# Batch 2 of a dilated sliding-window attention: crossing all eight heads by DMA and computing them in four quadrant visits

## The chip, the cores and the metric

The kernel runs on one core of a Trainium2 chip. A core has a matrix engine (PE, with its weight loads shown apart as PEld), a vector engine (DVE), a scalar engine (ACT), a general engine (POOL) and a sync engine (SP), each with its own instruction queue that is worked off strictly in order. POOL and SP also start DMA transfers. The metric is the device time of one execution in microseconds (us); lower is better. The kernel before takes 291.92 us, the median of 3 runs (291.9 to 294.13).

## What is computed

The input is q, k and v of shape (8 batches, 8 heads, 576 positions, 64) and two weight matrices. Heads 0 to 3 attend to the last 32 positions, heads 4 to 7 to every fourth of the last 128. The result, as a 4608 by 512 matrix, goes through a feed-forward layer with squared ReLU.

```python
rel = pos[:, None] - pos[None, :]
mask_plain = (rel >= 0) & (rel < window)                                        # window = 32, heads 0..3
mask_dil = (rel >= 0) & (rel < window * dilation) & (rel % dilation == 0)       # dilation = 4, heads 4..7
scores = np.where(masks, scale * np.matmul(q, k.transpose(0, 1, 3, 2)), -1e9)
attn = softmax(scores)
x = np.matmul(attn, v)            # then (batch, position) by (head, dim): 4608 x 512
h = np.maximum(x @ w_in, 0.0)     # 512 x 2048
out = h * h @ w_out               # 2048 x 512
```

## The kernel before, in words

Everything is written out by hand in one order, and each engine takes its share of that order. The backbone is the feed-forward layer. Its PE work is cut into groups, numbered g = 0, 1, 2 and so on. Tokens come in tiles: four tiles of 256 tokens with 16 groups each (groups 0 to 63), then tiles of 512 tokens with 32 groups each (from group 64). Of the tile of tokens 768 to 1023, groups 48 to 55 are the first product (line 912, eight results u0 to u7), groups 56 to 63 the second (line 960). Each result of a first product sits in one of the four PSUM buffers called pf until ACT evicts it with the ReLU (line 925); DVE then squares it (line 930 or 889). A matmul of a later result waits for the buffer of the result four before.

Between the groups stand the steps of the attention. Batches and heads are counted from 0, so the third batch is batch 2 (the name XB in the code) and the fourth is batch 3 (NATURAL). Two heads form a pair e: pairs 0 and 1 are plain, 2 and 3 dilated. Two lists say what is issued behind which group: PROGRAM, whose cells between the bars belong to one group each, and the list `steps`, sorted by group and then by a small priority.

The batches are treated in different ways. Batch 1 is transposed on PE: a code such as 1q2 (line 284) turns q of pair 2 into PSUM, and copies spread it into qT and, block by block, into the block-diagonal key tile kbd (lines 304 to 321). Codes a and b compute scores, exponential and mask of a pair's two parts (lines 358 to 369), o and p its value product and normalisation (lines 421 to 436); a digit in front is the batch. From batch 3 on nothing is transposed on PE. Four DMA transposes on SP (line 264, code x) bring q and k of all heads into the tiles qx and kx; copies put them where PE wants them (`arrange`: R, the ends of the dilated pairs; K, the plain pairs' keys; Q, their queries), and PE then works in four quadrants of its array at once, in visits (line 621, code V: pairs for scores, then pairs for values). After a visit come E (exponential on ACT, line 658, then mask on DVE), L (logarithm of the sums on ACT, lines 634 to 640) and X (exponential of its negative on ACT, line 644, then the products on DVE, lines 647 and 649). A visit with values of one pair is followed by four logarithms, one with values of two pairs by two for each.

Batch 2 is a mixture before the change. Its dilated heads are crossed by DMA and computed in quadrants: V022,23 for the scores behind group 56, and the value products with the next batch's first scores behind group 59. Its plain pairs are transposed on PE (2q0, 2k0, 2q1, 2k1) and computed by a, b, o and p behind groups 39 to 56.

The loads come from POOL in the order of the codes L: q and k (line 197), v (codes p, d and r, lines 218 to 239). Eight semaphores are used in turn, so that a load waits for the one eight before it. SP's queue holds the DMA transposes and the stores of results (line 852), also in order.

The two lines below, from `quadrants` and the group's eviction, show the shared buffers:

```python
main_s = [ps_a.tile([P, 512], f32, name="pa") for _ in range(2)]
nc.scalar.activation(hv, acc[u][:, :].rearrange("p (x n) -> p x n", x=2), ACT.Relu)
```

Of the kernel before, what the change touches and what calls it, by code (L numbers as in the profile page):

```python
# [12 lines left out]
RES = 4  # L13
# [68 lines left out]
def kernel(  # L82
# [118 lines left out]
    def crossed(b: int, e: int):  # L201

        return int(b == XB and e == 3 or b >= NATURAL and e == 1)

    def load_v(b: int, parts, which="pdr"):
# [8 lines left out]
        for what in which:  # L214
            if what == "p":
                for e in range(NE // 2):
                    for hl, rows in sides:
                        nc.gpsimd.dma_start(  # L218
                            dst[rows, e, i0:i1, rows],
                            v[b, 2 * e + hl, 64 * i0 : 64 * i1, :].rearrange("(i p) d -> p i d", p=64),  # L220
                        )
# [14 lines left out]
            elif b == XB:  # L236
                for g, rows in sides:
                    for i in (0, 8):
                        nc.gpsimd.dma_start(
                            dst[rows, NE // 2 : NE, i, rows],  # L240
                            v[b, H // 2 + g : H - g : 3 - 2 * g, 64 * i : 64 * i + 64, :].rearrange("h p d -> p h d"),
# [19 lines left out]
    def cross(b: int, nm: str, part: int):  # L261

        n, m0, h0 = MN[part], MS[part], H // 2 if b == XB else 0
        nc.sync.dma_start_transpose(
            (qx if nm == "q" else kx)[b % 2][:, h0:, :, m0 : m0 + n].rearrange("p h c m -> p (h c) m"),
            staged(b, nm)[0:n, part, h0:, :].rearrange("p h x -> p (h x)"),
        )

    def trans(b: int, e: int, nm: str, part: int, home: str):
# [5 lines left out]
        if b == 2:  # L275
            m0, n, pitch, cuts = 0, M, M, [(t[0:80, a, :, :], MS[a], 80) for a in range(2)]
        else:

            m0, n, pitch, cuts = MS[part], MN[part], 80, [(t[0:80, part, :, :], 0, 80)]
# [160 lines left out]
    def step(b: int, code: str):  # L440
# [6 lines left out]
        if what in "qk" and (b > XB or b == XB and e >= NE // 2):  # L447
            t = (qx if what == "q" else kx)[b % 2]
            halves(e, what, t[:, 2 * e : 2 * e + 2, :, :], 0, M, copier(what, e, home), his)
        elif what in "qQkK" and "h" in home:  # L450
# [37 lines left out]
    def arrange(b: int, what: str, g: int, jj: int, copy=nc.vector.tensor_copy):  # L488
# [6 lines left out]
        if what == "Q":  # L495
            nc.vector.tensor_copy(q_both[rows, :, jj::2, :], qx[b % 2][src, 0:n, :, :])
# [126 lines left out]
    def natural_step(b: int, code: str):  # L623
# [28 lines left out]
        else:  # L652
# [6 lines left out]
            mask = (mask_f if e >= NE // 2 else mask_n)[:, 0:n]  # L659
# [207 lines left out]
    def ffn_groups(tk0: int, nt: int):  # L867
# [7 lines left out]
        kts = (2, 3, 0, 1) if tk0 >= 3 * NT else (0, 2, 1, 3) if NT <= tk0 < 2 * NT else (0, 1, 2, 3) if tk0 in (0, 2 * NT) else (2, 3, 0, 1)  # L875
# [271 lines left out]
    def run(code):  # L1147
        if code == "y":
            for nm in "qk":
                nc.gpsimd.memset(staged(1, nm)[64:80, 0, :, :], 0.0)  # L1150
                nc.gpsimd.memset(staged(2, nm)[64:80, 0, 0 : H // 2, :], 0.0)
# [40 lines left out]
    COMBINE = {17: "10", 18: "20", 22: "11 21", 61: "40", 62: "41", 63: "30 31"}  # L1192
# [11 lines left out]
    for x, code in enumerate(("R00", "R01", "R10", "R11")):  # L1204
        steps.append((48 + x, 1, XB, code))
    steps.append((56, 2, XB, "V022,23/"))
# [83 lines left out]
```

## Time and profile before

| what | value |
|---|---|
| median of 3 runs | 291.92 us (291.9 to 294.13) |
| profiled execution, whole | 292.3 us |
| its span | 290.5 us |
| instructions in the span | 8181 |
| DMA | 83125 packets, 35.45 MB, mean 122 GB/s |
| stage of batch 2, groups 40 to 63 | 60.21 to 88.94 us of the span |

The span runs from the first to the last instruction of one profiled execution; the time of a run is a little longer. Each line of the profile that is quoted below names an engine, a line of the kernel, the operation, and the tile written from the tile read. In a timeline the first column is the start in us of the span, the second the time from the first start to the last end of the instructions that the row merges, and xN their number; what stands in square brackets is idle time of the engine ahead of them. In a list of groups the columns after the count are busy time in us, mean duration of one in ns, and idle time ahead. Instructions of one engine overlap a little, so a row's cost is often read from one start to the next.

### The profile page before, as it was taken

Reading aid. Unit: us, or ns where it says so; the run is one execution under the profiler, and the core shown is the slowest. Engines: PE = TensorE matmul, PEld = TensorE weight load, DVE = VectorE, ACT = ScalarE, POOL = GpSimd, SP = SyncE. Lnnn points to the kernel's source line nnn. Section 1 sums busy time; section 2 is a strip of 40 time slices with the busy share of each in tenths; the row PEclk is TensorE's granted clock in tenths of the full one; section 3 lists DMA queues with packets and bytes.
Section 4 is the critical chain, followed back from the end, with each engine's and each line's share of the span. In section 5 each row is a group of like instructions: output and inputs, shape, how many; then the busy total and the mean of one; then the engine's idle time right before and its main releaser. Section 6 shows DMA issues by size and latency. Waiting matters only on the chain.

```text
span 290.5 us, 8181 instructions
## 1 busy us (share of the span) xinstructions
PE 280.7 (97%) x3321; PEld 200.4 (69%) x3341; DVE 207.0 (71%) x447; ACT 194.7 (67%) x419; POOL 130.0 (45%) x210
## 2 busy tenths in 40 slices
PE   8879999999999999999999999999999999999994
PEld 3569855977955578557865786578657865885683
DVE  2565496798877997869786978697869545742762
ACT  7688748877986886597669766976697456306610
POOL 8569965393892779584043467950000000000000
PEclk9999999999999999999999999999999999999999
DMA  7999999999999987999789998740310040013013
GB/s 112 200 158 212 210 159 201 211 157 200 164 152 179 153 113 80 230 207 132 97 146 215 164 162 163 82 27 2 101 47 2 2 148 0 0 47 100 0 38 108
DMA packets 83125, 35.45 MB, mean 122 GB/s; under 512 B 52624, under 2 KB 78480, under 8 KB 83088
## 3 DMA queue, kind: packets, MB, share of 16 engines
q0 software_dynamic: 49280, 18.43, 55.9%
q1 hardware_dynamic: 33008, 16.10, 27.9%
q10 hardware_dynamic: 800, 0.41, 0.6%
q8 instruction: 26, 0.43, 0.6%
q14 instruction: 11, 0.09, 0.1%
HBM read 37.40 MB, written 9.44 MB: 161 GB/s over the span
## 4 chain that ended last, share of the span: by engine, by line
PE 88%; DMA 5%; DVE 2%; POOL 2%; issue 1%; ACT 1%; ACTq 0%; POOLq 0%
PE pf L912 41%; PE pf L997 29%; PE pf L960 8%; DMA w_in<-in_moe_w_in_dram 3%; DMA kb<-in_k_dram 2%; PE po L621 2%; PE pa L621 1%; PE pa L284 1%; PE pf L621 1%; PE pd L621 1%; POOL qb L197 1%; PE pa L358 1%; PE po L421 1%; DVE kbd L507 1%; PE pd L423 0%
## 5 line engine op out<-in xcount | busy, mean ns | idle before, releaser
L912 PE MATMUL pf<-xT,w_in 128*128 128x512 bf16 (+1 forms) x693 | 128.7, 340 | 2.1 <-DMA w_in<-in_moe_w_in_dram 1.4
L912 PEld LDWEIGHTS <-w_in 128*128 128x128 bf16 x704 | 77.4, 113 | 46.1 <-DMA w_in<-in_moe_w_in_dram 1.5
L925 ACT ACTIVATE h2T<-pf 128x512 bf16<-128x512 f32 x144 | 83.0, 600 | 36.7 <-PE pf L912 36.4
L997 PEld LDWEIGHTS <-h2T 128*128 128x128 bf16 x688 | 65.3, 98 | 9.1
L997 PE MATMUL pf<-w_out_sb,h2T 128*128 128x256 bf16 x440 | 52.3, 273 | 0.0
L483 POOL DMA_DIRECT2D vbd<-in_v_dram x80 | 43.4, 564 | 13.6 <-DMA qb<-in_q_dram 4.2
L889 DVE TENSOR_TENSOR h2T<-h2T 128x2048 bf16<-128x2048 bf16 (+2 forms) x42 | 35.6, 867 | 16.2 <-ACT h2T L925 15.6
L1008 DVE TENSOR_TENSOR osb<-pf,osb 128x512 f32<-128x512 f32 (+1 forms) x35 | 23.5, 673 | 12.6 <-PE pf L997 11.8
L960 PE MATMUL pf<-w_out_sb,h2T 128*128 128x512 bf16 x119 | 29.5, 379 | 0.6 <-issue 0.3
L647 DVE TENSOR_TENSOR xT<-po,rec 128x512 bf16<-128x512 f32 x16 | 11.0, 688 | 15.8 <-ACT rec L644 11.2
L197 POOL DMA_DIRECT2D qb<-in_q_dram x18 | 13.1, 730 | 16.3 <-DMA xx<-qb 15.0
L960 PEld LDWEIGHTS <-h2T 128*128 128x128 bf16 x128 | 11.4, 98 | 10.8
L930 DVE TENSOR_TENSOR h2T<-h2T 128x1024 bf16<-128x1024 bf16 (+1 forms) x20 | 11.5, 585 | 7.7 <-ACT h2T L925 7.2
L658 ACT ACTIVATE pt<-pa 128x384 bf16<-128x384 f32 (+1 forms) x32 | 15.3, 496 | 1.7 <-DVE xT L649 1.1
L475 POOL DMA_DIRECT2D vbd<-in_v_dram x20 | 12.3, 626 | 8.4 <-DMA kb<-in_k_dram 4.2
L644 ACT ACTIVATE rec<-rec 128x576 f32<-128x576 f32 x22 | 15.0, 682 | 0.5
L218 POOL DMA_DIRECT2D vbd<-in_v_dram x16 | 10.9, 690 | 9.7 <-DMA kb<-in_k_dram 4.4
L470 POOL DMA_DIRECT2D vd<-in_v_dram x20 | 12.3, 623 | 4.0 <-DMA kb<-in_k_dram 3.1
L997 PE MATMUL pf<-w_diff,s2T 128*128 128x256 bf16 x112 | 13.7, 273 | 0.0
L997 PE MATMUL pf<-vbd,h2T 128*128 128x256 bf16 x112 | 13.4, 273 | 0.0
L197 POOL DMA_DIRECT2D kb<-in_k_dram x18 | 13.0, 722 | 0.7 <-DMA vd<-in_v_dram 0.7
L997 PE MATMUL pf<-w_diff,h2T 128*128 128x256 bf16 x104 | 13.3, 273 | 0.0
(160 smaller groups left out, 416.6 us busy)
## 6 DMA issues: line engine op xcount, KB each, us to landing
out_dram<-osb SPq DMA_DIRECT2D x18, 128.0 KB, 5.8
qb<-in_q_dram POOLq DMA_DIRECT2D x7, 320.0 KB, 8.1
kb<-in_k_dram POOLq DMA_DIRECT2D x7, 320.0 KB, 10.3
vd<-in_v_dram POOLq DMA_DIRECT2D x32, 64.0 KB, 6.9
w_in<-in_moe_w_in_dram POOLq DMA_DIRECT2D x4, 512.0 KB, 8.4
w_out_sb<-in_moe_w_out_dram POOLq DMA_DIRECT2D x4, 512.0 KB, 11.0
qb<-in_q_dram POOLq DMA_DIRECT2D x7, 256.0 KB, 7.0
kb<-in_k_dram POOLq DMA_DIRECT2D x7, 256.0 KB, 12.3
```

The source lines that it names most:

```text
L197: nc.gpsimd.dma_start(t[0:n, part, hs, :], src[b, hs, t0 : t0 + RES * n, :].rearrange("h (p r) d -> p h (r d)", r=RES))
L470: nc.gpsimd.dma_start(vds[b][rows, e, :, :], v[b, H // 2 + 2 * e + hl, 0:512, :].rearrange("(m p r) d -> p m (r d)", p=64, r=RES),)
L483: nc.gpsimd.dma_start(v_rows[b % 2][p0 + 16 * r : p0 + 16 * r + 16, e, :, :], v[b, 2 * e + hl, :, :].rearrange("(i m r) d -> r m i d", r=R ...
L621: nc.tensor.matmul(out, lhs, rhs, start=begin, stop=True, skip_group_check=True)
L644: nc.scalar.activation(rec[:, :], rec[:, :], ACT.Exp, scale=-1.0)
L658: nc.scalar.activation(pt, sp[b, e][g][:, 0:n], ACT.Exp, scale=SCALE)
L889: nc.vector.tensor_tensor(out=hv, in0=hv, in1=hv, op=ALU.mult)
L912: nc.tensor.matmul(to, w_in_sb[piece][:, kt, c0 : c0 + 509 : 4], rhs, start=(kt == kts[0] and x == 0), stop=(kt == kts[-1] and x == per - ...
L925: nc.scalar.activation(hv, acc[u][:, :].rearrange("p (x n) -> p x n", x=2), ACT.Relu)
L960: nc.tensor.matmul(cur[m][:, :], h2[:, m // 2 if per == 1 else hh, HF * (f % 2) + f // 2, P * x : P * x + P], w_out_sb[:, f, :], start=(f ...
L997: nc.tensor.matmul(bank(nm, m, c.start)[:, m, c], a[:, k, P * m : P * m + P], w[:, c], start=begins, stop=(k == HF - 1), skip_group_check= ...
L1008: nc.vector.tensor_tensor(out=to[:, at, c], in0=src[:, at, c], in1=other[:, at, c], op=ALU.add)
```

## The change

All heads of batch 2 are now crossed by DMA, 16 blocks in each transpose instead of 8. The PE transposes and the part-by-part scores and value products of its plain pairs are gone, and with them two memsets on POOL. Instead the batch has four quadrant visits: behind group 49 the scores of pair 2; behind group 52 the scores of pair 3 and the values of pair 2; behind group 55 the scores of both plain pairs and the values of pair 3; behind group 60 the values of both plain pairs and the first scores of batch 3. The end copies follow groups 47 and 48, the key copies (eight, in another layout than later batches') groups 49 and 51 on DVE, and the four query copies groups 50, 51 and 53, on ACT. Batch 3's end copies move behind group 59, all on DVE. The dilated and then the plain values of batch 2 are loaded in another order: the dilated ones first, then batch 3's q and k, then the plain ones, with the heads of pair 1 swapped. The 512-token tile from token 1024 takes its channels in the order 2, 3, 0, 1 instead of 0, 1, 2, 3, and the weight differences of code 30 and 31 come one group later. In the diff, "a" behind a copy's code gives it to ACT.

```diff
...
-    "1k3 1o0 1o1f | 1a3 1Q0 | 1K0 1o3 | 1Q1 1K1 | 1Q2 | 1b0 | | 1Q3 1K2 L2:vwp L3:q00123 L3:q10123 L2:vwdr | "
-    "L2:x | | 2q0 | | 2k0 1V2 | 1b2 1p0 | 1b1 1V3 1K3 | L3:x | 1p2 1p1f | 2a0 1b3 | 2k1l 2b0 2o0 1p3f 2k1h | 2q1 "
-    "| | 2p0 L3:Vd0 L4:q00123 L4:q10123 L3:V1 2a1 | 2b1 | | 2o1 | | | 2p1f | | | | L4:x | | | | | | | | | | | | "
...
+    "| 1a0 1a1 | 1k3 1o0 1o1f | 1a3 1Q0 | 1K0 1o3 | 1Q1 1K1 | 1Q2 | 1b0 |  | 1Q3 1K2 L2:vwdr L3:q00123 L3:q10123 "
+    "L2:vwp | L2:x |  |  |  | 1V2 | 1b2 1p0 | 1b1 1V3 1K3 | L3:x | 1p2 1p1f | 1b3 | 1p3f |  |  | L3:Vd0 L4:q00123 "
+    "L4:q10123 L3:V1 |  |  |  |  |  |  |  |  |  | L4:x |  |  |  |  |  |  |  |  |  |  |  |  |  |  |  |  |  | L4:V "
...
     def crossed(b: int, e: int):
 
-        return int(b == XB and e == 3 or b >= NATURAL and e == 1)
+        return int(b >= XB and e == 1)
...
-                            v[b, 2 * e + hl, 64 * i0 : 64 * i1, :].rearrange("(i p) d -> p i d", p=64),
+                            v[b, 2 * e + (hl ^ crossed(b, e)), 64 * i0 : 64 * i1, :].rearrange("(i p) d -> p i d", p=64),
...
-                            v[b, H // 2 + g : H - g : 3 - 2 * g, 64 * i : 64 * i + 64, :].rearrange("h p d -> p h d"),
+                            v[b, H // 2 + g : H : 2, 64 * i : 64 * i + 64, :].rearrange("h p d -> p h d"),
...
     def cross(b: int, nm: str, part: int):
 
-        n, m0, h0 = MN[part], MS[part], H // 2 if b == XB else 0
+        n, m0 = MN[part], MS[part]
         nc.sync.dma_start_transpose(
-            (qx if nm == "q" else kx)[b % 2][:, h0:, :, m0 : m0 + n].rearrange("p h c m -> p (h c) m"),
-            staged(b, nm)[0:n, part, h0:, :].rearrange("p h x -> p (h x)"),
+            (qx if nm == "q" else kx)[b % 2][:, :, :, m0 : m0 + n].rearrange("p h c m -> p (h c) m"),
+            staged(b, nm)[0:n, part, :, :].rearrange("p h x -> p (h x)"),
...
-        if b == 2:
-            m0, n, pitch, cuts = 0, M, M, [(t[0:80, a, :, :], MS[a], 80) for a in range(2)]
-        else:
-
-            m0, n, pitch, cuts = MS[part], MN[part], 80, [(t[0:80, part, :, :], 0, 80)]
+        m0, n, pitch, cuts = MS[part], MN[part], 80, [(t[0:80, part, :, :], 0, 80)]
...
-        if what in "qk" and (b > XB or b == XB and e >= NE // 2):
-            t = (qx if what == "q" else kx)[b % 2]
-            halves(e, what, t[:, 2 * e : 2 * e + 2, :, :], 0, M, copier(what, e, home), his)
-        elif what in "qQkK" and "h" in home:
+        if what in "qQkK" and "h" in home:
...
         if what == "Q":
-            nc.vector.tensor_copy(q_both[rows, :, jj::2, :], qx[b % 2][src, 0:n, :, :])
+            copy(q_both[rows, :, jj::2, :], qx[b % 2][src, 0:n, :, :])
+        elif what == "K" and b == XB:
+            for c in range(2):
+                nc.vector.tensor_copy(
+                    k_both[rows, g::2, :, 2 * c + jj :: RES].rearrange("p i h m -> p h i m"),
+                    kx[b % 2][src, 0:n, c, :].rearrange("p h (i m) -> p h i m", m=16)[:, :, g::2, :],
+                )
...
-            mask = (mask_f if e >= NE // 2 else mask_n)[:, 0:n]
+            mask = (mask_f if e >= NE // 2 else mask_n if b > XB else mask_p[:, 384:])[:, 0:n]
...
-        kts = (2, 3, 0, 1) if tk0 >= 3 * NT else (0, 2, 1, 3) if NT <= tk0 < 2 * NT else (0, 1, 2, 3) if tk0 in (0, 2 * NT) else (2, 3, 0, 1)
+        kts = (0, 1, 2, 3) if tk0 == 0 else (0, 2, 1, 3) if NT <= tk0 < 2 * NT else (2, 3, 0, 1)
...
                 nc.gpsimd.memset(staged(1, nm)[64:80, 0, :, :], 0.0)
-                nc.gpsimd.memset(staged(2, nm)[64:80, 0, 0 : H // 2, :], 0.0)
...
-    COMBINE = {17: "10", 18: "20", 22: "11 21", 61: "40", 62: "41", 63: "30 31"}
+    COMBINE = {17: "10", 18: "20", 22: "11 21", 61: "40", 62: "41", 64: "30 31"}
...
-    for x, code in enumerate(("R00", "R01", "R10", "R11")):
-        steps.append((48 + x, 1, XB, code))
-    steps.append((56, 2, XB, "V022,23/"))
-    steps += [(57, 1, XB, f"E{e}{x}") for e in (2, 3) for x in range(2)]
-    for b in range(NATURAL, B):
+    for b in range(XB, B):
         t = G * (b - 1)
-        early = b == NATURAL
+        early = b <= NATURAL
...
-        start = 59 if early else t - 8
+        def copies(codes, *at, act=0):
+            steps.extend((y, 1, b, code + "a" * (x >= len(at) - act)) for x, (code, y) in enumerate(zip(codes.split(), at)))
+
+        ends_, keys, queries = "R00 R01 R10 R11", "K00 K01 K10 K11", "Q00 Q01 Q10 Q11"
+        if b == XB:
+            copies(ends_, 47, 47, 48, 48)
+            visit(49, [(b, 2)], [])
+            expo(2, 50, 50)
+            copies(keys, 49, 49, 51, 51)
+            visit(52, [(b, 3)], [(b, 2)])
+            norm(2, 52)
+            copies(queries, 50, 51, 53, 53, act=4)
+            expo(3, 53, 53)
+            visit(55, [(b, 0), (b, 1)], [(b, 3)])
+            norm(3, 57)
+            for e in range(2):
+                expo(e, 56 + e, 56 + e)
+            visit(60, [(b + 1, 2)], [(b, 0), (b, 1)])
+            norm(0, 60)
+            norm(1, 61)
+            continue
+        expo(2, *((t, t + 2) if early else (t - 1, t + 1)))
         second = t + (7 if early else 5)
-        if early:
-            visit(start, [(b, 2)], [(XB, 2), (XB, 3)])
-            for e in (2, 3):
-                steps.extend([(start + e - 2, 3, XB, f"L{e}"), (start + e - 1, 0, XB, f"X{e}")])
-        expo(2, *((start + 4, start + 7) if early else (start + 7, start + 9)))
...
-        for x, code in enumerate(("R00", "R01", "R10", "R11")):
-            steps.append(((57, 57, 54, 55)[x] if early else t - 11, 1, b, code + "a" * (b > NATURAL and x > 1)))
-        for x, code in enumerate(("K00", "K01", "K10", "K11", "Q00", "Q01", "Q10", "Q11")):
-            steps.append((t + x if early else t - 6 + x, 1, b, code))
+        copies(ends_, *([59] * 4 if early else [t - 11] * 4), act=0 if early else 2)
+        copies(keys, *(t + x if early else t - 6 + x for x in range(4)))
+        copies(queries, *(t + 4 + x if early else t - 2 + x for x in range(4)))
```

10 rows, old and new, of the table PROGRAM are left out of this document.

## The prediction

> **What bounds the kernel now.** I read the page's busy shares and chain first. The profiled execution took 292.3 us, of which the span is 290.5 us; the other 1.8 us lie around it and I leave them alone. The median of the runs shown is 291.92 us, so a difference worked out on this execution is set against 292.3 us and then taken 0.4 us lower.
>
> ```profile
> PE 280.7 (97%) x3321; PEld 200.4 (69%) x3341; DVE 207.0 (71%) x447; ACT 194.7 (67%) x419; POOL 130.0 (45%) x210
> PE 88%; DMA 5%; DVE 2%; POOL 2%; issue 1%; ACT 1%; ACTq 0%; POOLq 0%
> ```
>
> PE is the bound almost everywhere: it works 97% of the span and makes 88% of the chain. After the first 28 us its waits sum to some 0.3 us. So a microsecond of PE work removed is a microsecond won, and a microsecond that PE stands still is lost for good: nothing behind it has slack to give it back. But what can PE be made to wait for? The stage in question runs from 60 to 89 us, and the windows of its middle answer:
>
> ```profile
> 70.00:75.00 5.00, 5.00 (x84) 4.93 (x82) 4.18 (x13) 4.59 (x12) 3.15 (x6) 1.00 1.73 188
> 75.00:80.00 5.00, 5.00 (x60) 4.80 (x58) 3.99 (x11) 4.94 (x13) 4.18 (x8) 1.00 1.13 170
> 80.00:85.00 5.00, 4.79 (x142) 2.99 (x144) 4.80 (x17) 4.03 (x10) 4.97 (x9) 1.00 1.18 155
> ```
>
> The columns after the window's length are PE, PEld, DVE, ACT and POOL. ACT is busy 13.56 of these 15 us: its 67% over the span hides a stage in which it is nearly full. The change puts work on it just here.
>
> **PE work.** From PE's timeline, batch 2 now costs: four pairs of transposes (q and k of pairs 0 and 1) at 0.29 us, 1.16; their scores 0.16 + 0.22 twice, 0.77; their value products 0.31 + 0.45 twice, 1.53; the visit V022,23 0.70 (81.04 to 81.74); the visit V032/22,23 1.50 (84.20 to 85.70). Sum 5.66 us. The four new visits: scores of one dilated pair alone 0.40 (the 0.29 us tail of the visit at 95.94 plus its 0.1 us of issue); scores of one and values of one dilated pair 0.65 (95.94 to 96.59); scores of both plain and values of a dilated pair 0.87 (105.36 to 106.23); values of both plain pairs with scores of the next batch's 1.07 (113.32 to 114.39). Sum 2.99. **PE saves 2.67 us**, if it never waits.
>
> **ACT work.** Removed: eight query copies from PSUM (four of 0.4 us in each of two runs of 1.6), scores' exponentials and normalisations of the plain pairs. Added: four query copies for all heads at once, since the new code gives all four to ACT. The trace has no such copy on ACT from the crossed tile, but it has the same shape on ACT and the same copy on DVE:
>
> ```profile
> L304 ACT COPY qT<-pa 64x288 bf16<-64x288 bf16 x8 | 3.1, 392 | 0.4 <-PE pa L284 0.3
> L1096 ACT COPY vbd<-kbd 64x1152 bf16<-64x1152 bf16 x2 | 2.3, 1149 | 0.0
> L496 DVE COPY qT<-xx 64x1152 bf16<-64x1152 bf16 x20 | 9.4, 468 | 0.4
> ```
>
> I take 1.15 us, the row of the same engine and shape; the lower end is DVE's 0.47, the upper 4 x 0.39 = 1.56. Four cost 4.6 us. Each single-pair visit is also followed by four logarithms instead of two:
>
> ```profile
> 96.78 0.22 ACT L639 ACTIVATE rec<-pa 64x64 f32<-64x64 f32 x1
> 96.91 0.58 ACT L640 ACTIVATE rec<-pd 64x512 f32<-64x512 f32 x1
> 97.50 0.22 ACT L639 ACTIVATE rec<-pa 64x64 f32<-64x64 f32 x1
> 97.62 0.58 ACT L640 ACTIVATE rec<-pd 64x512 f32<-64x512 f32 x1
> 98.22 0.60 ACT L925 ACTIVATE h2T<-pf 128x512 bf16<-128x512 f32 x1
> 98.72 0.68 ACT L644 ACTIVATE rec<-rec 128x576 f32<-128x576 f32 x1
> ```
>
> By start to start, that is 1.44 us for the logarithms, 0.5 for an eviction (a pair at 99.29 takes 1.08), 0.57 for the exponential. A dilated pair's two score exponentials take 0.80 (four in 1.61 from 81.99), two plain pairs' four take 1.77 (from 106.18).
>
> **Walking through the stage.** Group 48 starts at 71.19 now. Ahead of it 1.56 us of PE steps go, so 69.63. But those steps stood between batch 1's last scores (1b3) and their value product (1p3f), and covered exponential and mask; only group 47 is left there, and I charge 0.5 us of waiting. Group 48 starts at 70.15, group 49 (1.31 us like 48) ends at 72.8.
>
> Visit 1 then needs all four end copies of batch 2. On DVE they stand behind 1p3f's product. That ends at 73.27 now, 2.08 us after group 48's start, of which 0.4 went to another normalisation (that of 2o0) on ACT, which is gone: 71.9. Two of the copies are these four lines:
>
> ```profile
> 74.28 0.19 DVE L504 COPY kbd<-xx 64x128 bf16<-64x128 bf16 x1
> 74.39 0.30 DVE L507 COPY kbd<-xx 64x128 bf16<-64x128 bf16 x1
> 74.70 0.19 DVE L504 COPY kbd<-xx 64x128 bf16<-64x128 bf16 x1
> 74.81 0.31 DVE L507 COPY kbd<-xx 64x128 bf16<-64x128 bf16 x1
> ```
>
> 0.42 us each, four 1.7, done at 73.6. Visit 1 runs from 73.65 to 74.05, a wait of 0.8 us; before, seven groups lay between these copies and their visit. Group 50 lets ACT start evicting at 74.45, after standing idle from about 71.4.
>
> From there ACT works without a gap, in this order up to the exponentials that visit 3 needs: evictions u0, u1 1.08; E2 0.80; a query copy 1.15; u2, u3 1.08; a query copy 1.15; u4 0.54; L2 1.44; u5 0.54; X2 0.57; two query copies 2.30; E3 0.80. **Sum 11.45 us, so 85.9**; the masks on DVE (0.35) make it 86.3. PE has for the same stretch groups 50 to 55 (0.87 for two short ones, 3.46 for four) and visit 2 (0.65, which itself waits 0.9 us for E2 and its mask, to 76.75): it reaches visit 3 at 80.1 and **stands 6.2 us**. Visit 3 ends at 87.2. Then E0 and E1 1.77, L3 1.44, X3 0.57 on ACT reach 91.1; the products on DVE 1.08 (100.13 to 101.21) free the banks at 92.2. PE has done groups 56 to 60 (0.865 each) by 91.5; visit 4 runs to 93.3, groups 61 to 63 to 95.9. Group 64 starts at 88.94 now. **Loss: 7.0 us.** Tile 2 now begins with channels 2 and 3, so its wait for the plain pairs' X1 (about 97) falls at group 66 (97.6) and is hidden.
>
> DVE gains eight key copies (320 or 256 elements) and loses the eight transposed ones of 288 from PSUM (0.48 us each). By that row the first four end at 75.5, when the first eviction pair does, and the last four run while ACT is the one late: nothing.
>
> **Does PE lose speed by standing?** The trace bounds this from both sides:
>
> ```profile
> 1.07 3.65 PE L676 MATMUL po<-kbd 128*128 128x512 bf16 x10 [1.07 <-DVE kbd L1091]
> 21.36 2.81 PE L912 MATMUL pf<-xT,w_in 128*128 128x256 bf16 x24 [1.42 <-DMA w_in<-in_moe_w_in_dram]
> ```
>
> The kernel's first ten matmuls need 3.65 us; at the later pace (0.216 start to start) they would need 2.33, so 1.3 us are lost. After a gap of 1.42 us nothing is lost (24 at 0.11). The granted clock reads 1.00 in both places, so it does not show this. A stand of 6.2 us is over four times the harmless gap; I take the start's price, 1.3 us, of which 0.4 is covered by visit 4's wait for ACT: 0.9. [...]
>
> **Queues and transfers.** SP's four transposes of batch 2 carry 16 blocks instead of 8. The half crossing ran from 54.42 to its last landing at 64.7 (10.3 us); batch 3's full one, in similar traffic, from 68.70 to about 83 (14.3). At the latter batch 2's lands at 68.7, ahead of 71.9; at twice the former at 75.0, 3.1 us late. I take the full row, the same shape. POOL loses two memsets of 0.94 us at 30 us (no PE wait there to shorten: nothing) and issues batch 3's q and k behind eight transfers instead of four, some 2.1 us later; their crossing's end copies are wanted on DVE behind X3, 92 instead of 81, so this is hidden, as are batch 2's plain values (issued by about 69, wanted at 92).
>
> **Rivals.**
> - *Slow ACT queue, PE slowed after its stand* (forecast): 292.3 + 7.0 + 0.9 - 0.4 = 299.8. Chance 0.50.
> - *The same, PE at full pace*: 298.9. For it: the harmless gap; against it: the stand is far longer. 0.27.
> - *Crossing late*: the end copies wait for q's second transpose, and everything behind moves by up to 3.1 us: 302.9. For it: the DMA share is above 1 at 54 to 70 us. Against it: batch 3's row. 0.11.
> - *PE stays the bound, and is faster*: ACT's queue keeps ahead of visit 3, so the saved 2.67 us come out: 289.3. It decides where ACT's 11.45 us up to E3 come under the 5.65 us that PE has from its first eviction to visit 3. Even query copies at 0.47 us would leave 8.7. 0.07 for this; 0.05 for something near the old time.
>
> **Numbers.** The range 296.5 to 302.5 takes in the first two cases with the copies' cost 0.6 us either way each and part of the late crossing; it leaves out the last cases. A change within 1% (2.9 us) is about what a measurement of this kernel cannot tell from none. Faster 0.07, within 1% 0.05, slower 0.88.
>
> **What would show it.** A row qT<-xx of 64x1152 on ACT, four at about 1.15 us; PE idle of about 6 us ahead of the visit with the plain scores, put down to the mask or to ACT; ACT full from 74 to 91; tile 2's first matmul near 96.8; matmuls of groups 56 to 58 at about twice 0.216 us apart; the rest of the trace moved as a whole. I am wrong if visit 3 starts within 2 us of group 55's end, or if the end copies start after 72.5 because a transpose landed late.

## The result

The changed kernel takes 300.73 us (median of 4 runs, 300.48 to 306.09), the kernel before 291.97 us in the same session. The ratio is 1.028, with a 95% interval of 1.022 to 1.034: the change makes the kernel slower by some 8.8 us, where 299.8 us was forecast. The execution profiled first was a disturbed one (306.09 us at a mean clock of 0.97; the other three have a median of 300.56 us, and differences below are taken to these), so the profile below is of another execution of the same changed kernel, which took 301.49 us with a span of 299.7 us.

The busy shares and the chain, from the page of the changed kernel:

```profile
PE 283.7 (95%) x3327; PEld 199.8 (67%) x3345; DVE 208.0 (69%) x449; ACT 197.5 (66%) x417; POOL 128.1 (43%) x208
PE 85%; DMA 5%; ACT 4%; issue 2%; POOL 1%; DVE 1%; DVEq 0%; ACTq 0%; POOLq 0%
```

ACT had 1% of the chain before and has 4% now. PE's share fell although PE's busy time grew by 3 us. The windows of the stage, in the same columns as before (length, PE, PEld, DVE, ACT, POOL, the granted clock of PE, DMA share, GB/s):

```profile
70.00:75.00 5.00, 4.60 (x64) 4.21 (x64) 3.22 (x12) 1.63 (x4) 1.63 (x3) 1.00 1.57 207
75.00:80.00 5.00, 4.29 (x82) 3.80 (x81) 3.64 (x9) 4.98 (x9) 3.10 (x6) 1.00 1.86 132
80.00:85.00 5.00, 0.61 (x6) 0.34 (x4) 2.36 (x6) 4.89 (x9) 3.35 (x7) 0.99 1.20 173
85.00:90.00 5.00, 3.57 (x72) 2.28 (x74) 3.06 (x8) 4.28 (x11) 4.73 (x9) 0.50 1.17 163
90.00:95.00 5.00, 5.00 (x74) 2.34 (x76) 3.22 (x12) 2.14 (x5) 2.65 (x6) 0.82 1.46 191
```

ACT is idle for most of the first window and full in the next two. In the third window PE works 0.61 of 5 us. In the fourth it works again, at half the clock (0.50). The ACT rows and the PE rows around it show why (start, length, engine, line; in brackets the idle time ahead and who ended it):

```profile
74.56 1.08 ACT L924 ACTIVATE h2T<-pf 128x512 bf16<-128x512 f32 x2 [2.92 <-PE pf L911]
...
82.14 0.68 ACT L643 ACTIVATE rec<-rec 128x576 f32<-128x576 f32 x1
82.85 2.31 ACT L489 COPY qT<-xx 64x1152 bf16<-64x1152 bf16 x2
85.18 0.87 ACT L657 ACTIVATE pt<-pa 128x384 bf16<-128x384 f32 x2
```

```profile
70.50 2.79 PE L911 MATMUL pf<-xT,w_in 128*128 128x256 bf16 x24
...
73.97 0.22 PE L620 MATMUL pa<-kbd 64*64 64x64 bf16 x2 [0.39 <-DVE kbd L506]
74.12 2.13 PE L911 MATMUL pf<-xT,w_in 128*128 128x256 bf16 x16
76.91 0.19 PE L620 MATMUL po<-pt,vd 64*64 64x80 bf16 x1 [0.67 <-DVE pt L659]
...
86.21 0.24 PE L620 MATMUL po<-pt,vd 64*64 64x80 bf16 x1 [5.60 <-DVE pt L659]
```

Behind group 55 PE stands 5.60 us until the third pair's exponentials, last in ACT's row, are masked. Group 64, the first rows of the next tile (before, then after), starts at 97.91 us instead of 88.94, which is 9.0 of the 9.2 us by which the span grew:

```profile
88.94 7.07 PE L912 MATMUL pf<-xT,w_in 128*128 128x512 bf16 x32
...
97.91 4.31 PE L911 MATMUL pf<-xT,w_in 128*128 128x512 bf16 x19
```

To split that loss I take the stretch from the same feed-forward row (24 matmuls, at 57.30 us before and 57.50 after) to group 64, by start times in PE's timeline:

| us | before | after |
|---|---|---|
| PE waits (after: 0.35, 0.39, 0.67, 5.60) | 0 | 7.01 |
| attention steps of both batches on PE | 8.43 | 7.09 |
| second products, groups 56 to 63 | 6.89 | 8.81 |
| the other feed-forward rows (remainder) | 16.32 | 17.50 |
| sum | 31.64 | 40.41 |

So 7.0 of 8.8 us are waits, and 1.9 are second products, of which nine run at half clock (0.427 us apart instead of 0.216). Of what PE saves in attention steps (1.34 us) it loses 1.18 us again in the last row.

One kind of row is easily taken for a wait. Behind a visit the profile shows 0.16 us of idle time put down to "issue" (0.22 at the lower clock), twice before and twice after, and each time lists one second product too few: 11 and 15 before, 19 and 11 after, where the program has 12, 16, 20 and 12. In the kernel with two query copies in ACT's gap all 12 behind the last visit are listed, and no idle time:

```profile
95.54 2.54 PE L959 MATMUL pf<-w_out_sb,h2T 128*128 128x512 bf16 x11 [0.16 <-issue]
```

```profile
93.16 2.76 PE L959 MATMUL pf<-w_out_sb,h2T 128*128 128x512 bf16 x12
```

So this time is counted as the matmul that is not listed.

### The profile page after: what moved, and what is told of

It reads as the page before. It is cut to its first block, busy times and chain, and to the rows that moved or that the text cites. A ratio compares the mean times of both kernels' runs of the same rounds, so it can differ in the third digit from the quotient of the medians.

```text
span 304.3 us, 8182 instructions
## 1 busy us (share of the span) xinstructions
PE 287.9 (95%) x3327; PEld 202.4 (67%) x3345; DVE 208.1 (68%) x449; ACT 197.5 (65%) x417; POOL 128.0 (42%) x208
## 4 chain that ended last, share of the span: by engine, by line
PE 80%; DMA 8%; ACT 6%; DVE 2%; issue 1%; POOL 1%; SPq 0%; DVEq 0%; ACTq 0%; POOLq 0%
PE pf L911 38%; PE pf L996 27%; PE pf L959 5%; DMA xx<-qb 5%; DMA kb<-in_k_dram 3%; PE po L620 2%; ACT qT L489 1%; PE pa L620 1%; ACT h2T L924 1%; ACT pt L657 1%; PE pf L620 1%; ACT rec L643 1%; PE pd L620 1%; PE pa L280 1%; POOL qb L197 1%
## 5 line engine op out<-in xcount | busy, mean ns | idle before, releaser
L911 PE MATMUL pf<-xT,w_in 128*128 128x512 bf16 (+1 forms) x693 | 131.6, 346 | 0.7
L911 PEld LDWEIGHTS <-w_in 128*128 128x128 bf16 x704 | 78.8, 115 | 46.8 <-issue 1.2
L959 PE MATMUL pf<-w_out_sb,h2T 128*128 128x512 bf16 x121 | 30.4, 386 | 0.6 <-issue 0.4
L646 DVE TENSOR_TENSOR xT<-po,rec 128x512 bf16<-128x512 f32 x18 | 12.4, 689 | 15.9 <-ACT rec L643 11.7
L657 ACT ACTIVATE pt<-pa 128x384 bf16<-128x384 f32 (+1 forms) x36 | 17.1, 498 | 2.3 <-DVE xT L648 1.0
L643 ACT ACTIVATE rec<-rec 128x576 f32<-128x576 f32 x24 | 16.4, 681 | 0.6
L639 ACT ACTIVATE rec<-pd 64x512 f32<-64x512 f32 x24 | 13.9, 580 | 0.0
L996 PE MATMUL pf<-vbd,h2T 128*128 128x256 bf16 x112 | 13.4, 273 | 0.0
```

Of the source, the lines that this page charges most:

```text
L639: nc.scalar.activation(rec[to, 0:512], d[at, :], ACT.Ln)
L643: nc.scalar.activation(rec[:, :], rec[:, :], ACT.Exp, scale=-1.0)
L657: nc.scalar.activation(pt, sp[b, e][g][:, 0:n], ACT.Exp, scale=SCALE)
L911: nc.tensor.matmul(to, w_in_sb[piece][:, kt, c0 : c0 + 509 : 4], rhs, start=(kt == kts[0] and x == 0), stop=(kt == kts[-1] and x == per - ...
L959: nc.tensor.matmul(cur[m][:, :], h2[:, m // 2 if per == 1 else hh, HF * (f % 2) + f // 2, P * x : P * x + P], w_out_sb[:, f, :], start=(f ...
L996: nc.tensor.matmul(bank(nm, m, c.start)[:, m, c], a[:, k, P * m : P * m + P], w[:, c], start=begins, stop=(k == HF - 1), skip_group_check= ...
```

## Experiments

Each kernel is the changed kernel with the edit shown; where a minus line already has an experiment's edit, the kernel is built on that experiment, which the text names. The kernel before ran beside each set, at 291.94 (first four runs), 292.79 (next four), 291.72 (next three) and 292.18 us (last). I compare sets by the ratio to it.

### The changed kernel once more

> The changed kernel once more, for a profile of an undisturbed execution. If the queue of ACT makes the loss, visit 3 (plain scores) starts at about 86 with PE idle some 6 us ahead of it, and the four query copies take 1.15 us each. If the crossing makes it, the end copies start well after 72 and the wait ahead of visit 1 is the larger one. If the clock takes part, the granted clock is below 1 somewhere behind a long wait. Time about 300.6 us.

Measured: 301.49 us, the profile above. The four query copies on ACT took 1.147 to 1.151 us each, visit 3 starts at 86.21 us behind the long wait, the end copies start at 72.08 us without a wait for DMA, and the clock is at 0.50 behind the long wait.

### The query copies on DVE

```diff
-            copies(queries, 50, 51, 53, 53, act=4)
+            copies(queries, 50, 51, 53, 53)
```

> The four query copies of batch 2 on DVE instead of ACT, nothing else. Theory ACT queue: the 11.45 us of ACT work up to the exponentials of visit 3 lose 4.6, the wait ahead of visit 3 falls by about as much and gets too short to slow PE: 4.5 to 5.5 us faster than the changed kernel, about 295.5 us. Rival late crossing (end copies wait for the transposes and everything behind is moved): the copies stand behind that wait, so 0 to 1 us, about 300 us.

Measured: 296.81 us (296.74 to 298.33), ratio 1.0156 (1.0086 to 1.0226): some 3.7 us of the loss are gone. The copies take 0.44 to 0.47 us each on DVE. Rows of DVE and of PE:

```profile
80.46 0.46 DVE L648 TENSOR_TENSOR xT<-pa,rec 64x64 bf16<-64x64 f32 x2
80.96 0.94 DVE L489 COPY qT<-xx 64x1152 bf16<-64x1152 bf16 x2
81.93 0.63 DVE L659 TENSOR_TENSOR pt<-pt,mask_f 128x384 bf16<-128x384 bf16 x2
```

```profile
82.43 0.19 PE L620 MATMUL po<-pt,vd 64*64 64x80 bf16 x1 [2.89 <-DVE pt L659]
```

The wait ahead of visit 3 is halved. ACT's queue with these copies was therefore the largest cause found. But 2.89 us stay, with the last two copies now ahead of the masks on DVE. The forecast of 295.5 us was 1.3 us too good.

### PE kept busy through its wait

```diff
+FILL = 28
...
+    zero = const.tile([P, P], bf16, name="zero")
...
+                    for _ in range(FILL if (tk0, f, kt) == (3 * NT // 2, NF - 1, kts[-1]) else 0):
+                        nc.tensor.matmul(
+                            acc[u][:, :], zero[:, :], xT[:, 0, 0:512], start=False, stop=False, skip_group_check=True
+                        )
...
+            nc.gpsimd.memset(zero[:, :], 0.0)
```

The matmuls use weights of zero, which POOL writes at the kernel's start, and add nothing to the last result of group 55.

> 28 matmuls of 512 columns with a zero weight tile are added to the last result of group 55, ahead of visit 3, where PE stands anyway (28 x 0.216 = 6.0 us); they change no value. Theory slowed clock: PE comes out of the wait at full pace, 0.9 us faster than the changed kernel, about 299.7 us. Rival clock without effect: the same time, or a little slower where the fill outlasts the wait, 300.6 to 301.2 us.

Measured: 299.78 us (299.44 to 300.37), ratio 1.025 (1.017 to 1.033). The filling row of PE (27 of the 28 are listed) with the wait inside visit 4, and the windows:

```profile
79.81 5.99 PE L910 MATMUL pf<-xT,zero 128*128 128x512 bf16 x27
...
93.45 0.22 PE L622 MATMUL pa<-kbd 64*64 64x64 bf16 x2 [0.65 <-DVE kbd L508]
```

```profile
85.00:90.00 5.00, 4.95 (x88) 2.63 (x88) 3.02 (x8) 4.69 (x12) 5.00 (x9) 1.00 1.19 161
90.00:95.00 5.00, 4.01 (x92) 2.42 (x92) 3.70 (x13) 2.88 (x6) 1.98 (x4) 1.00 1.43 180
```

The clock stays at 1.00, and visit 3 takes 0.86 us instead of 1.75 (start to start). The lowered clock costs the changed kernel 0.8 us (300.56 - 299.78): a small difference, but all four runs here (299.44 to 300.37) lie below the three of the changed kernel that the result is taken to (300.48 to 300.90). Its rows lose more than that, 0.9 us in visit 3 and 1.6 us in the second products (8.81 against 7.16 us here), but at full clock visit 4 comes sooner and waits 0.65 us for the fourth batch's end copies.

### The fourth batch's q and k loaded later

```diff
-    "... 1Q3 1K2 L2:vwdr L3:q00123 L3:q10123 L2:vwp | L2:x | | | | 1V2 | ..."
+    "... 1Q3 1K2 L2:vwdr L2:vwp | L2:x | | | | 1V2 L3:q00123 L3:q10123 | ..."
```

> Batch 3's q and k loads are issued four groups later, behind batch 2's crossing instead of beside it. Theory late crossing: the last transpose lands up to 4 us earlier, the end copies start earlier by what they waited for it, and the kernel gets faster by as much, 1 to 3 us (298 to 299.5 us). Theory ACT queue alone, with the crossing in time: the same within 0.5 us, about 300.6 us.

Measured: 301.01 us (300.01 to 301.65), ratio 1.028 (1.021 to 1.036): no gain. POOL was itself late, so these loads moved only behind four more transfers (from 62.5 to 66.2 us). The third batch's end copies ran right behind pair 3's product of batch 1, with no wait for DMA. The crossing was shorter in this execution: its last transpose is issued at 61.63 us and lands 8.3 us later, 14.3 us after the first issue at 55.59, where the changed kernel's takes 16.9 us (54.60 to 71.5, the last one issued at 60.69 and landing 10.8 us later). That need not come from the edit, for with the query copies on DVE it took 13.4. It was in time in both, in the changed kernel by 0.6 us.

### Two query copies in ACT's gap

```diff
-            copies(queries, 50, 51, 53, 53, act=4)
+            copies(queries, 48, 48, 53, 53, act=4)
```

> The changed kernel with one move: the first two of the third batch's four query copies stay on ACT but go to step 48, ahead of the evictions, where ACT stood idle for 2.92 us (until 74.56 us) in the changed kernel's profile; the last two stay where they are. ACT-queue theory (visit 3's masks come late because ACT has more to do than time before it, and a gap it did not use): two copies of 1.15 us fill the gap, everything behind them on ACT comes 2.3 us earlier, PE's wait ahead of visit 3 falls from 5.6 to some 3.3 us, and the time from 300.7 to about 298.4 us. Rival (what counts is the DVE's and the crossing's part of the chain, ACT merely waits with it): 300 us or above. A second rival: the copies wait there for the crossing and hold up the evictions behind them; then 301 to 302 us.

Measured: 299.14 us (298.37 to 299.37), ratio 1.021 (1.0165 to 1.0255), which is 1.4 us less than the changed kernel by the times and 2.0 by the ratios. ACT's row and the visit:

```profile
71.49 2.30 ACT L489 COPY qT<-xx 64x1152 bf16<-64x1152 bf16 x2
74.37 1.09 ACT L924 ACTIVATE h2T<-pf 128x512 bf16<-128x512 f32 x2 [0.58 <-PE pf L911]
```

```profile
83.84 0.24 PE L620 MATMUL po<-pt,vd 64*64 64x80 bf16 x1 [3.56 <-DVE pt L659]
```

The copies fill the gap and hold nothing up. Visit 3's wait falls by 2.0 us, and the time by most of that. This is the ACT queue again, shown by order alone.

### ... and the other two on DVE

```diff
-            copies(queries, 48, 48, 53, 53, act=4)
+            copies("Q00 Q01", 48, 48, act=2)
+            copies("Q10 Q11", 53, 53)
```

> As the run before, and the last two query copies on DVE at step 53. Against the kernel with all four copies on DVE (296.8 us) DVE has two copies of 0.45 us fewer ahead of the third pair's masks. If DVE's row of work between 73 and 82 us, which has hardly a gap in that kernel, is what sets visit 3 there: 0.9 us less, 295.9 us. If the exponentials' place behind pair 2's normalisation sets it (the ACT row waited 1.11 us for the product on DVE): 296.3 to 296.8 us.

Measured: 298.04 us (297.01 to 300.24), ratio 1.019 (1.013 to 1.025). Visit 3 waited 2.79 us, against 2.89 with all four on DVE. DVE has 0.9 us less to do ahead of the masks and gains nothing by it: between its squares it now waits 0.43 and 0.32 us for ACT. The expectation of 295.9 us failed. Neither engine alone sets visit 3. ACT waited 0.88 us for pair 2's product on DVE, and that product started at 79.91 us, just when ACT's exponential for it (79.88) and DVE's square (79.90) had ended.

### Exponentials ahead of the normalisation

```diff
-            norm(2, 52)
+            norm(2, 53)
-            copies("Q10 Q11", 53, 53)
+            copies("Q10 Q11", 54, 54)
```

> As the run before, and on ACT the third pair's two exponentials go ahead of pair 2's four logarithms and its reciprocal instead of behind them; the last two query copies go one step later. The normalisation (four logarithms 1.44 us, exponential 0.67 us, products on DVE 1.1 us) then no longer stands between visit 2 and these exponentials, but visit 3 still needs its result, for it takes the same accumulator banks. If the order counts: 1 to 1.5 us less than the run before, about 294.6 us. If the normalisation itself is the longer arm to visit 3: no more than 0.5 us less.

Measured: 298.62 us (297.98 to 298.96), ratio 1.0197 (1.016 to 1.0235): no gain. PE's rows name the new wait:

```profile
82.93 0.19 PE L620 MATMUL po<-pt,vd 64*64 64x80 bf16 x1 [3.20 <-DVE xT L646]
84.28 0.36 PE L620 MATMUL pa<-qT,kbd 64*64 64x96 bf16 x16 [0.68 <-DVE qT L489]
```

Visit 3 needs pair 2's product too, for that frees the accumulator banks po and pd. The order only exchanged the one wait for the other.

### Visits 3 and 4 later

```diff
-            visit(55, [(b, 0), (b, 1)], [(b, 3)])
+            visit(57, [(b, 0), (b, 1)], [(b, 3)])
...
-            visit(60, [(b + 1, 2)], [(b, 0), (b, 1)])
+            visit(61, [(b + 1, 2)], [(b, 0), (b, 1)])
```

Their exponentials and normalisations move along (58, 61, 62), and the fourth batch's end copies go to 58. The other edits are those of the run before.

> As the run before, and visit 3 two groups of products later (57), the plain pairs' exponentials at 58, visit 4 one group later (61), with the fourth batch's end copies at 58, ahead of pair 3's product instead of behind it. If PE's waits come from the visits' places among PE's own work, PE now has two groups (2.06 us) more to do ahead of visit 3 and its wait there goes: 1 to 1.5 us less than the run before, 293.3 us. If the chain visit 2, normalisation, visit 3, exponentials, visit 4, normalisation sets the time of group 64 whatever PE does meanwhile: within 0.5 us of the run before, and the wait turns up ahead of visit 4 or of group 64's last pairs.

Measured: 297.40 us (297.33 to 298.20), ratio 1.0164 (1.013 to 1.020), 1.2 us below the run before. PE, which now has groups 56 and 57 ahead of visit 3:

```profile
82.81 0.19 PE L620 MATMUL po<-pt,vd 64*64 64x80 bf16 x1 [1.47 <-DVE xT L646]
...
90.07 0.20 PE L620 MATMUL po<-pt,vbd 64*64 64x96 bf16 x1 [0.26 <-DVE xT L646]
```

Visit 3 starts only 0.12 us earlier than in the run before, although two groups of PE's work (eight matmuls, 1.73 us from start to start) now lie ahead of it. Its time is set by the row of copies, logarithms and products, and PE's groups only fill the wait, which falls by the same 1.73 us. PE does not have to do these groups later; 0.95 us of it come back as waits ahead of visit 4 (0.26) and within group 64's tile (0.69).

### The query copies on POOL

```diff
-            copies(queries, 50, 51, 53, 53, act=4)
+            copies(queries, 48, 48, 48, 48, act=4)
...
-            arrange(b, what, e, int(code[2]), nc.scalar.copy if code[3:] else nc.vector.tensor_copy)
+            arrange(b, what, e, int(code[2]), (nc.gpsimd.tensor_copy if what == "Q" else nc.scalar.copy) if code[3:] else nc.vector.tensor_copy)
```

> The changed kernel with the four query copies of the third batch on neither ACT nor DVE: on POOL, at step 48, ahead of its issues of the fourth batch's values. DVE's row of work between 73 and 82 us is then 1.8 us shorter than with the copies on DVE, ACT's 4.6 us shorter than in the changed kernel; POOL's own price is in no trace so far (its fill of 16x1024 took 0.94 us, so a copy of 64x1152 is put at 1 to 1.5 us, 4 to 6 us in all from about 71 us), and the fourth batch's loads come that much later, which the later visits have room for. Theory (the row visit 2, normalisation, exponentials, visit 3, exponentials, visit 4, normalisation sets group 64, and copies count only where they stand in that row): 1 us less than with the copies on DVE, so a ratio to the kernel before of about 1.012, 295.5 us where that is 292. Copies are the whole loss: 292 us or below. POOL is too slow or its loads are late: above 297 us.

Measured: 299.07 us (298.42 to 299.93), ratio 1.025 (1.023 to 1.028). A miss, for a reason that I had not listed. Rows of POOL and of DVE:

```profile
69.93 4.88 POOL L489 COPY qT<-xx 64x1152 bf16<-64x1152 bf16 x4 [2.83 <-DMA xx<-qb]
```

```profile
71.86 0.46 DVE L503 COPY kbd<-xx 64x128 bf16<-64x128 bf16 x1
...
72.56 1.04 DVE L503 COPY kbd<-xx 64x128 bf16<-64x128 bf16 x1
...
73.84 1.02 DVE L503 COPY kbd<-xx 64x128 bf16<-64x128 bf16 x1
```

POOL needs 1.22 us a copy. While it runs, DVE's copies of line 503, which take 0.18 to 0.19 us in the changed kernel, take up to 1.04 us. The end copies therefore take 3.7 us in all instead of 1.8, and visit 1 waited 2.0 us for them. Two of them last 1.04 and 1.02 us, most of one of POOL's 1.22. The copies of line 506, which lie between them, take 0.29 to 0.33 us, against a median of 0.30 in the changed kernel. Why the one kind gets longer beside POOL's copies and the other does not, no run shows. Visit 3's wait fell to 1.99 us all the same, so the copies' place in the row does count. The row also dates the crossing in this run: it was issued from 54.29 us on, and POOL's wait for the last transpose ended at 69.93.

### Normalisation first again, copies ahead of it

```diff
-            norm(2, 53)
+            norm(2, 52)
-            copies("Q10 Q11", 54, 54)
+            copies("Q10 Q11", 51, 51)
```

This is built on the kernel with visits 3 and 4 later; the visits stay at 57 and 61.

> The kernel with the visits at 57 and 61 again, and two orders put back or moved: pair 2's logarithms and product ahead of the third pair's exponentials, and the last two query copies on DVE ahead of that product (step 51) instead of behind it. In the run before it (visits at 57 and 61) visit 3 waited for the product on DVE until 82.8 us and then 0.7 us more for the query copies. If the row visit 2 to visit 3 is what counts, the product comes at about 80.5 us, visit 3 at 81.5 us, and the time is 1.3 to 2 us below that run: ratio about 1.010 to 1.012, 295 to 295.5 us where the kernel before is 292. If the time is set behind visit 3 (its exponentials, the end copies, visit 4): within 0.5 us of that run, ratio 1.015 to 1.017.

Measured: 297.91 us (296.47 to 299.01), ratio 1.021 (1.017 to 1.024): nothing gained. In the profiled execution (299.01 us), DVE and PE:

```profile
87.28 0.43 DVE L503 COPY kbd<-xx 64x128 bf16<-64x128 bf16 x1 [1.79 <-DMA xx<-qb]
...
89.65 0.69 DVE L646 TENSOR_TENSOR xT<-po,rec 128x512 bf16<-128x512 f32 x1
```

```profile
82.28 0.19 PE L620 MATMUL po<-pt,vd 64*64 64x80 bf16 x1 [0.98 <-DVE pt L659]
...
90.40 0.24 PE L620 MATMUL po<-pt,vbd 64*64 64x96 bf16 x1 [3.36 <-DVE xT L646]
```

Visit 3 came 0.5 us earlier. But the fourth batch's end copies, put ahead of pair 3's product, waited on DVE for that batch's crossing and held the product and visit 4 up. This execution is the slowest of the four (the fastest took 296.47 us), so the wait need not be as long in the others.

### The plain values first

```diff
-    "... 1Q3 1K2 L2:vwdr L3:q00123 L3:q10123 L2:vwp | L2:x | ..."
+    "... 1Q3 1K2 L2:vwp L3:q00123 L3:q10123 L2:vwdr | L2:x | ..."
```

> The changed kernel with one part of the change undone: the plain pairs' values of the third batch are issued ahead of the fourth batch's q and k again (the two-row values go behind instead). The prediction put this part at nothing, hidden by POOL's spare time. So: within 0.7 us of the changed kernel's 300.7 us (ratio 1.025 to 1.030). If the order of the loads matters, the two-row values, which visit 2 needs at about 76 us, come late: 1 us or more above.

Measured: 304.66 us (303.31 to 307.14), ratio 1.043 (1.040 to 1.046): some 4 us above the changed kernel. PE's rows in the profiled execution (307.14 us, the slowest of the four), and one of POOL:

```profile
75.83 0.34 PE L620 MATMUL pa<-xx 64*64 64x80 bf16 x16 [1.69 <-DMA xx<-qb]
...
85.29 0.26 PE L620 MATMUL po<-pt,vbd 64*64 64x64 bf16 x1 [4.30 <-DMA vbd<-in_v_dram]
```

```profile
76.40 0.59 POOL L239 DMA_DIRECT2D vbd<-in_v_dram  x1 [4.88 <-DMA kb<-in_k_dram]
```

Visit 2 waits 4.3 us for the dilated heads' values, which stand last in POOL's order: POOL itself stood 4.88 us there until one of the fourth batch's loads had landed. And the crossing too lands late, 20 us after its first issue at 55.45.

### The fourth batch's scores apart

```diff
-            visit(61, [(b + 1, 2)], [(b, 0), (b, 1)])
+            visit(61, [], [(b, 0), (b, 1)])
+            visit(63, [(b + 1, 2)], [])
```

The end copies of that batch go to 60; the rest is as in the kernel with the normalisation first.

> The run before it (pair 2's normalisation first, visits at 57 and 61) with one part taken out of visit 4: the fourth batch's first scores are a small visit of their own behind group 63, and its end copies go behind pair 3's product on DVE (step 60) instead of ahead of it. In the run before, these copies waited on DVE for the fourth batch's crossing until 87.28 us and held pair 3's product up until 89.65 us; visit 4 waited 3.4 us for that product and, at the slowed clock, ended at about 92.4 us. Theory (the row through visits sets group 64, and its last link but one is the fourth batch's crossing, in which the third batch has no part): pair 3's product comes at 87.8 us, visit 4 at 88.4 us, its results at 93 us, group 64 at 91.6 us with its last pairs at 93 us; 2 to 3 us less than that run, ratio to the kernel before about 1.010 to 1.014. If the ratio stays at 1.018 or above, something behind visit 4 sets the time instead. No reading has it at or below the kernel before, for the waits ahead of visits 1, 2 and 3 (1.8 us together) stay.

Measured: 298.75 us (297.68 to 299.97), ratio 1.024 (1.019 to 1.028). PE:

```profile
88.69 0.20 PE L620 MATMUL po<-pt,vbd 64*64 64x96 bf16 x1 [1.51 <-DVE xT L646]
...
93.07 0.22 PE L620 MATMUL pa<-xx 64*64 64x80 bf16 x2 [1.24 <-ACT osb L967]
94.13 0.33 PE L620 MATMUL pa<-xx 64*64 64x80 bf16 x14 [0.83 <-DVE xT L648]
94.42 7.10 PE L911 MATMUL pf<-xT,w_in 128*128 128x512 bf16 x32
```

Up to visit 4 this went as expected: it starts at 88.69 us, and its wait is down from 3.36 to 1.51 us. But the split-off scores then wait for PSUM: a visit takes both pa banks, and in these lie the plain pairs' end results until DVE has multiplied them (its last products end at 92.97 and 94.07 us; for the first of the two waits the profile names ACT's copy of another result instead). Group 64 starts at 94.42 us. The expected 2 to 3 us did not come.

No order that I tried is as fast as the kernel before. The best two, the query copies on DVE (1.0156) and the visits later (1.0164), can't be told apart; the first is the simpler. What takes the rest of the loss away, no run shows.

## Why the prediction was right

**The sum.** 299.8 us against 300.73. Most of its links are in the trace: ACT's row from its first eviction to the exponentials that visit 3 needs was put at 11.45 us and measured 11.49 (74.56 to 86.05), the masks' end at 86.3 and visit 3 at 86.21, the stand at 6.2 and it was 5.60. The end copies on DVE were to end at 73.6 and ended at 73.91; ACT was to stand idle from about 71.4, and did from 71.64. That the total came so close has luck in it: the waits that the walk puts at 9.1 us (0.5, 0.8, 0.9, 6.2 and 0.7) came to 7.0, and PE's saving of 2.67 us came to some 1.1, and the two errors nearly cancel.

**PE saves 2.67 us: this step failed.** It holds only "if it never waits", and PE waits. The removed work was nearly right: 8.43 us in the table less the 2.80 of batch 1's steps are 5.63, of which 0.22 are a feed-forward matmul that the profile before doesn't list (it has 7 of the 8 of the row at 65.27 us). The forecast's 5.66 holds 0.32 us of the same kind, the idle rows behind its two visits. The new visits were put at 2.99. Those that PE enters without a wait cost what was forecast: visit 3 takes 0.86 us in the filled kernel (0.87 forecast), visit 4 takes 1.07 in the kernel with two query copies in ACT's gap (1.07 forecast). The two with a wait take more: 0.51 without its wait for visit 1 (0.40) and 0.89 for visit 2 (0.65), where 0.26 us pass between the first few matmuls and the rest, a gap that visit 3 of the filled kernel doesn't have. And the other feed-forward rows, which were taken as unchanged, took 1.2 us longer. Their matmuls are not slower; they follow each other at 0.109 and 0.216 us as before. Of the 1.2 us 0.22 are the unlisted matmul, some 0.5 are the ends of the three rows that run into a wait (the last matmul's end lies 0.16 us behind the time at which a next one would start), and 0.19 are a pause ahead of the ninth matmul behind visit 1, which starts at 75.21 us, when ACT's first eviction has ended at 75.16. Some 0.3 us stay open. At full clock PE thus saved about 1.1 us, and most of what is missing is the price of stopping and starting, which the forecast put at nothing. What the rival in which PE stays the bound would have given, no run shows, for PE waited ahead of visits in every kernel.

**ACT's copies.** 1.15 us each, as taken. Moved to DVE they give some 3.7 us back, and two of them in ACT's gap 1.4 to 2.0. The rest of the loss is not theirs. The prediction named it in its walk without pricing it apart: a row in which each visit hands over to ACT, ACT to DVE and DVE to the next visit. The experiments that shorten one link of that row found the next one beside it: the accumulator banks, the query copies, the fourth batch's end copies, the pa banks.

**Visit 4.** The walk had DVE free its banks at 92.2 us and the visit run at once. It left out that the fourth batch's first scores, which this visit also holds, need end copies that stand on DVE behind that product (1.7 us). In the filled kernel, which has the full clock that the walk assumed, visit 4 waits 0.65 us for them and group 64 starts at 96.6 us, put on the time of the kernel before by the row at 57.30; the walk said 95.9. Calling these copies hidden was wrong by that 0.7 us.

**Does PE lose speed by standing?** Yes, and the net price of 0.9 us was right: the fill gains 0.8. The remark that the granted clock does not show such a loss is wrong after a stand, where it reads 0.50 for 6.8 us. At the kernel's start, too, the matmuls follow each other at 0.427 us until 3.6 us and at 0.216 from 3.9 us on; the trace's record of the clock begins only at 3.77 us, so the 1.00 shown ahead of it is no reading.

**Queues and transfers.** The crossing's 14.3 us was 16.9 in the changed kernel, which leaves 0.6 us ahead of the end copies at 72.08; it was 13.4 with the query copies on DVE (53.76 to 67.2), 14.3 with the later loads and 15.6 with the copies on POOL. The rival of a late crossing is close: in the kernel with the plain values first the crossing took 20 us, and visit 1 waited for it. The new order of the loads was held to cost nothing, and as far as the later q and k go it does (moving them again changed nothing). But it is no indifferent part: undone alone it costs some 4 us.

**The chances.** The forecast's case, slow ACT queue and PE slowed after its stand, is the one that came. Faster had 0.07.

## What to carry to other kernels

When work leaves the bound engine for a second one, add up that second engine's queue in order, from the moment at which it can start to the instruction for which the bound engine waits; an average load of 67% says nothing about it. Where one stage hands over between three engines several times, a saved microsecond in one hand-over mostly turns up as a wait at the next, so look for the shared buffer or the queue neighbour behind each wait before moving anything. And count what is bundled with a step (here another batch's first scores in the same visit) as a condition of its start.

## What the runs showed of the hardware

**Half clock can come late, and here it lasted 3.4 us or twice or three times as long.** After two of the short stands the clock fell 0.4 to 0.5 us after PE had work again (84.47 against 84.06 us with the copies on POOL, 82.97 against 82.43 with the query copies on DVE); with the normalisation first it fell 0.3 us ahead of the end of a stand of 3.36 us (90.06 and 90.40 us, the first from the share 0.53 of the window from 90 to 91 us). In the kernel with the query copies on DVE PE stood from 79.54 to 82.43 us; its windows of 0.5 us (columns as above, the clock is the number ahead of the last two):

```profile
82.00:82.50 0.50, 0.07 (x4) 0.10 (x4) 0.50 (x3) 0.50 (x2) 0.50 (x2) 1.00 1.65 213
82.50:83.00 0.50, 0.50 (x38) 0.44 (x42) 0.50 (x3) 0.05 (x1) 0.50 (x2) 0.97 1.34 133
83.00:83.50 0.50, 0.50 (x46) 0.50 (x35) 0.23 (x1) 0.00 (x0) 0.33 (x2) 0.50 1.28 290
...
86.00:86.50 0.50, 0.50 (x3) 0.19 (x2) 0.00 (x0) 0.49 (x3) 0.50 (x2) 0.61 0.96 51
86.50:87.00 0.50, 0.50 (x4) 0.20 (x2) 0.00 (x0) 0.47 (x2) 0.50 (x1) 1.00 0.76 77
```

From the shares 0.97 and 0.61, the clock was at half from 82.97 to 86.39 us, 3.42 us. Worked out in the same way it was 3.42 us after a stand of 1.99 us (84.47 to 87.89, the copies on POOL), 3.41 after stands of 1.47 and 0.68 (84.05 to 87.46, visits later), and 6.83, twice as long, after the changed kernel's 5.60 (84.93 to 91.76). With the plain values first it was some 10.2 us, three times as long (78.6 to 88.8, from the shares 0.86 and 0.62 of windows of 5 us). Executions of one kernel differ in it: of the four with two query copies early and two on DVE, the mean clock was 1.000, 0.992, 0.989 and 0.989, and the times 297.01, 297.24, 298.84 and 300.24 us. How long a stand has to be for it, the runs do not settle: 1.99 us sufficed, and 1.47 and 0.68 close together, while the kernel before lost nothing after 1.42 us nor the last kernel after 1.51 (the clock stayed at 1.00 after both). So, by an estimate from these stretches, a stand of 2 us can already cost 1.7 us, half of the 3.4 us that PE then works at half clock.
